# Where a block's gradient rows are stored in the backward chain of a memory-augmented attention kernel

## The chip, the cores and the metric

The kernel runs on one core of one Trainium2 chip. A core has TensorE (PE, matrix products), VectorE (DVE), ScalarE (ACT), GpSimd (POOL) and SyncE (SP). SP computes nothing: it issues DMAs, one after another, in the order of its program. POOL issues DMAs too. The metric is the device time of one execution in microseconds (us); lower is better.

## What is computed

The reference is the forward pass of two summed branches and its gradients by automatic differentiation: a recurrent attention with a memory of 8 rows that is carried from one segment of 32 rows to the next, and a dense layer with a squared ReLU. The attention branch, cut to what matters (its gradient runs the same chain from the last segment to the first):

```python
for s in range(n_seg):                       # 2048 / 32 = 64 segments
    h = jnp.concatenate([mem, x[:, s*32:(s+1)*32, :]], axis=1)   # 8 + 32 rows of 512
    q, k, v = (jnp.einsum('btd,dhe->bhte', h, W) for W in (Wq, Wk, Wv))  # 32 heads of 128
    p = _softmax(jnp.where(mask, jnp.einsum('bhqe,bhke->bhqk', q, k) * scale, -1e9))
    o = jnp.einsum('bhte,hed->btd', jnp.einsum('bhqk,bhke->bhqe', p, v), Wo)
    mem = o[:, :M, :]
    outs.append(o[:, M:, :])
...
_out, _vjp = jax.vjp(_f, A_x, A_mem0, A_Wq, A_Wk, A_Wv, A_Wo, B_w1, B_b1, B_w2, B_b2)
_grads = _vjp(grad_out)
```

All inputs are bfloat16.

## The kernel before

The program runs in five parts one after the other: the dense branch, the forward chain over 64 segments, the backward pass of the memory rows of all blocks with the rest of the dense branch's weight gradients, the backward chain over 64 segments, and the weight gradients of the attention. The change lies in the backward chain.

One step of the backward chain is one segment. Four segments make a block (16 blocks), and the chain goes from the last block to the first. A step needs the gradient of the memory rows that the step before it made, so the steps are a chain. Within a step (`bwd`, L1314):

- `o0mm`, `o1mm`: the output gradient times Wo (L374), two halves of the heads; `o0ev`, `o0te` and so on: its casts and turns.
- `vp0`, `vp1` (L1384): gradient rows of the values; `vea`, `veb` (ACT) cast them into `G4["v"]`, called gv in the profile; `vla`, `vlb` cast the part that belongs to the memory rows.
- `s0`, `s1`, `d10` to `d41`: score gradients, on DVE.
- `kp0`, `kp1` and `qp0`, `qp1` (both L626, through `outer`): gradient rows of keys and queries. `kp` reads b_qN, the step's query rows; `qp` reads b_kN, its key rows, and b_kNL, the key rows of the block's memory (L1340, loaded once for each block in two halves by `ldk0`, `ldk1`; one buffer). `kea0` ... `qeb1` cast the results into `G4["k"]` and `G4["q"]`, gk and gq.
- `vg`, `kg`, `qg` (L495): these rows times the weights, summed over the heads into the gradient of the segment's rows.

gv, gk and gq hold the rows of all four steps of a block, in one buffer each. When a block is done they are stored whole in S_GB, for the last part of the program. Each is stored by two DMAs of 512 KB: the values by groups of heads, so that both DMAs need all eight heads of each group (`vo0`, `vo1`), keys and queries by heads 0 to 3 and 4 to 7 of each group (`ko0`, `ko1`, `qo0`, `qo1`). The next block's casts into the same buffer wait until the stores have read it.

The order is written out by hand. `B_ORDER` (L1156) has four strings, for the first to the last step of a block; `play` (L655) calls the named pieces in that order, and every engine keeps the order of the calls that fall to it. A plus sign shifts a name by one step; names with `L.` belong to a block and a plus shifts them by one block. In the first string, `L.ko1+` means the block that was finished with the step before; in the fourth string, `L.vo0++` means the block whose last step is running. `ldk0+++` in the first string loads b_kNL for the step that is running. Since no engine waits for another except through data, SP can run ahead of PE, and waits at the first DMA whose data or buffer isn't ready.

Other DMAs on SP's queue in a block's last step and in the next first step: `vtr` (L1344, a transposing load of b_vl, the next step's values), `L.ldt` (L635, the same for the memory's values, b_vTL), `L.qtr` (L1277, transposes b_gqL into gNat), `L.lq` (L1219, loads the next b_gqL into the same buffer), `L.qst` (L1286, stores gNat in S_GL), `L.sx` (L1289). On POOL's queue are `ldp`, `ldq`, `ldn` (L1330, L1337, L1338: b_P, b_qN, b_kN of a step), `ldv` and `ldk` (L1303 to L1308: PGD, b_gOL, b_GL, b_qNL of a block).

SP has eight semaphores for its DMAs, used in turn: each issue also waits until the DMA eight before it has landed.

Of the kernel before, what the change touches and what calls it, by code (L numbers as in the profile page):

```python
# [26 lines left out]
def kernel(  # L27
# [35 lines left out]
    L = M + SEG  # L63
# [146 lines left out]
    with sb("p1b", 2) as p1b, sb("p1", 1) as p1:  # L210
# [90 lines left out]
        for rb in range(NRB):  # L301
# [38 lines left out]
            xb = xq[rb]  # L340
# [310 lines left out]
    def on_engines(act, vec):  # L651

        return dict([(n, acp) for n in act.split()] + [(n, vcp) for n in vec.split()])
# [338 lines left out]
    with sb("la", 2) as la, sb("ls", 2) as ls, sb("lo", 1) as lo_, sb("wg", 2) as wg, psum("lpp", 1) as lpp, psum("lr", 4) as lr:  # L992
# [161 lines left out]


    B_ORDER = (  # L1156
# [6 lines left out]
        "pb+++ rb+++ ldq+++ L.H2+ ta+++ tb+++ vc+++ Ha+++ Hb+++ o0mm++++ o0ev++++ o1mm++++ o1ev++++ xb+++ o0fl++++ "  # L1163
# [10 lines left out]
        "ta++++ rb++++ Ha++++ tb++++ Hb++++",  # L1174
# [5 lines left out]
        "ta++++ L.qst+ kla1++++ tb++++ L.H0++ Ha++++ Hb++++")  # L1180
    ENGS = on_engines(
        "L.ra0 kea0 keb0 keb1 kla0 kla1 o0ev o1ev qea0 qea1 qeb0 ra vea veb vla vlb",
        "kea1 klb0 klb1 o0te o1te qeb1")
# [501 lines left out]
```

## Time and profile before

| | |
|---|---|
| median of 3 runs | 2894.07 us (2890.13 to 2901.47) |
| the profiled execution | 2889.67 us, of which the span 2887.9 us |
| granted clock of TensorE, mean over the span | 0.975 |
| busy share of the span | PE 93%, DVE 44%, ACT 35%, POOL 23% |
| moved by DMA | 586.77 MB, mean 203 GB/s |
| the queue of SP, share of 16 engines | 68.7% |
| the queue of POOL, share of 16 engines | 15.0% |
| the backward chain in the span | 1344.6 us (first o0mm) to about 2291 us |

The profile shows one execution. "Busy" is the time in which an engine ran instructions; the DMA share is the mean busy share of the core's 16 DMA engines. PEclk is the clock that TensorE was granted, 1.00 being full. A wait is told as the engine and line that waited, an arrow, and what ended it, with total us, number of times and the longest. In a timeline a line has its start, its length, the engine (SPq: SP's queue, that is issues of DMAs), the source line, the operation and out<-in; a bracket behind it tells how long the engine was idle before it.

### The profile page before, as it was taken

The numbers are of one execution on the slowest core, as the hardware profiler recorded it, in microseconds if no ns is written. First come the engines' busy times: TensorE is split into PE (matmuls) and PEld (weight loads), VectorE is DVE, ScalarE is ACT, GpSimd is POOL, SyncE is SP. The second block draws the span as 40 slices with busy tenths as digits, with TensorE's granted clock in tenths as the row PEclk, the third lists the DMA queues.
The fourth block names the chain that finished last, engine by engine and source line by source line (L and its number), as shares of the span: only waits on it lengthen the run. The fifth ranks groups of instructions, "written<-read, shape, count | busy, mean of one in ns | idle before, by whom it ended". The sixth has DMA issues, their size and how long they took to land.

```text
span 2887.9 us, 117038 instructions
## 1 busy us (share of the span) xinstructions
PE 2682.9 (93%) x52405; PEld 1446.5 (50%) x52405; DVE 1277.6 (44%) x3755; ACT 1002.5 (35%) x2330; POOL 662.5 (23%) x1284
## 2 busy tenths in 40 slices
PE   7998999999999997988998989989999898999999
PEld 3444555555555555455554545544554443444444
DVE  4544666666666664444454445544554401100000
ACT  2323444444444445232433333333433311111111
POOL 1001000000000001223443333433343323322221
PEclk9999999999999998998999999999999999999999
DMA  9764589899989998996677767786778799999993
GB/s 249 265 206 157 158 192 220 211 215 222 219 201 225 212 214 220 288 245 168 160 177 213 179 169 178 187 207 166 178 175 211 236 247 201 213 206 243 208 212 75
DMA packets 837275, 586.77 MB, mean 203 GB/s; under 512 B 637938, under 2 KB 723459, under 8 KB 833443
## 3 DMA queue, kind: packets, MB, share of 16 engines
q1 hardware_dynamic: 794642, 451.83, 68.7%
q0 software_dynamic: 41984, 127.32, 15.0%
q8 instruction: 411, 6.73, 1.0%
q14 instruction: 94, 0.76, 0.1%
q10 hardware_dynamic: 144, 0.13, 0.0%
HBM read 184.95 MB, written 248.79 MB: 150 GB/s over the span
## 4 chain that ended last, share of the span: by engine, by line
PE 78%; DMA 7%; SPq 6%; issue 4%; DVE 4%; ACT 1%; POOL 1%; ACTq 0%; DVEq 0%; POOLq 0%
PE ps_proj L374 15%; PE ps_gw L1643 14%; PE ps_gR L495 11%; PE ps_R L495 5%; SPq L1524 3%; PE ps_tr L167 3%; PE ps_L L374 3%; PE b_pp L626 3%; PE ps_RL L1254 3%; DMA b_qN<-S_A 2%; PE ps_sc L467 2%; PE f_pp L626 2%; PE ps_w L1104 2%; PE ps_B L345 2%; PE ps_gxb L354 2%
## 5 line engine op out<-in xcount | busy, mean ns | idle before, releaser
L1643 PE MATMUL ps_gw<-gn,HNc 128*128 128x512 bf16 x1920 | 422.1, 382 | 12.6 <-DMA gn<-S_GL 6.5
L1643 PEld LDWEIGHTS <-HNc 128*128 128x128 bf16 x1920 | 188.6, 98 | 240.7 <-issue 11.3
L422 ACT CAST f_N<-ps_proj 128x512 bf16<-128x512 f32 x320 | 184.1, 581 | 196.3 <-PE ps_proj L374 191.0
L1577 ACT CAST wt<-ps_gw 128x512 bf16<-128x512 f32 x128 | 73.8, 588 | 458.8 <-PE ps_gw L1643 419.7
L374 PEld LDWEIGHTS <-X 128*32 128x32 bf16 x5760 | 144.3, 96 | 136.7 <-DVE X L540 21.0
L1560 DVE TENSOR_TENSOR gx<-ps_rows,gb 128x512 f32<-128x512 f32 x16 | 11.1, 691 | 422.2 <-PE ps_rows L1558 422.2
L887 POOL COPY kM<-f_kT 128x256 bf16<-128x256 bf16 x64 | 25.8, 402 | 744.4 <-DVE f_kT L425 569.9
L495 PE MATMUL ps_gR<-Wv,gv 128*32 128x512 bf16 x2048 | 143.8, 402 | 6.8 <-issue 6.8
L495 PE MATMUL ps_gR<-Wk,gk 128*32 128x512 bf16 (+1 forms) x2048 | 139.4, 384 | 6.2 <-issue 5.2
L1643 PE MATMUL ps_gw<-GOc,gn 128*128 128x512 bf16 x640 | 139.2, 379 | 1.4 <-DMA GOc<-in_grad_out_dram 1.3
L495 PE MATMUL ps_R<-Wo,OT 128*32 128x256 bf16 x4096 | 128.6, 277 | 4.2 <-issue 2.8
L422 ACT CAST gON<-ps_proj 128x512 bf16<-128x512 f32 x128 | 75.0, 586 | 159.2 <-PE ps_proj L374 159.2
L1578 POOL DMA_DIRECT2D out_dram<-wt x120 | 64.9, 542 | 281.5 <-ACT wt L1577 266.3
L495 PE MATMUL ps_gR<-Wq,gq 128*32 128x512 bf16 (+1 forms) x2048 | 124.4, 351 | 5.0 <-issue 5.0
L374 PE MATMUL ps_proj<-Wo,GT 128*32 128x512 bf16 x2048 | 123.9, 384 | 5.3 <-DVE GT L1299 5.2
L374 PE MATMUL ps_proj<-Wq,X 128*32 128x512 bf16 x1920 | 127.3, 382 | 1.3 <-issue 1.3
L374 PE MATMUL ps_proj<-Wk,X 128*32 128x512 bf16 x1920 | 124.2, 382 | 1.1 <-issue 0.5
L422 ACT CAST gk<-b_pp 128x256 bf16<-128x256 f32 x192 | 69.2, 379 | 157.9 <-PE b_pp L626 96.4
L374 PE MATMUL ps_proj<-Wv,X 128*32 128x512 bf16 x1920 | 121.5, 378 | 0.0
L1335 POOL COPY PD<-b_P 32x320 bf16<-32x320 bf16 x256 | 115.4, 451 | 9.9 <-PE ps_tr L167 1.2
L1330 POOL DMA_DIRECT2D b_P<-S_A x63 | 33.8, 537 | 364.5 <-issue 136.1
L495 PEld LDWEIGHTS <-OT 128*32 128x32 bf16 x4096 | 104.6, 98 | 11.8 <-issue 5.7
(291 smaller groups left out, 5284.5 us busy)
## 6 DMA issues: line engine op xcount, KB each, us to landing
S_A<-f_N SPq DMA_DIRECT2D x64, 512.0 KB
out_dram<-wt POOLq DMA_DIRECT2D x134, 128.0 KB, 5.5
S_A<-f_N SPq DMA_DIRECT2D x64, 256.0 KB
S_GB<-gv SPq DMA_DIRECT2D x32, 512.0 KB
S_GB<-gk SPq DMA_DIRECT2D x32, 512.0 KB
S_GB<-gq SPq DMA_DIRECT2D x32, 512.0 KB
b_kN<-S_A POOLq DMA_DIRECT2D x63, 256.0 KB, 4.3
b_qN<-S_A POOLq DMA_DIRECT2D x63, 256.0 KB, 3.7
```

The costliest lines, as they stand in the source:

```text
L167: nc.tensor.transpose(ps_ap, in_ap, ident[base:base + k, base:base + k])
L345: nc.tensor.matmul(psB[:], lhsT=aT[:, fc, rc * P:(rc + 1) * P], rhs=W2[:, fc, :], start=(fc == 0), stop=(fc == FC - 1))
L374: nc.tensor.matmul(o, lhsT=hT[:, dc, :], rhs=x, start=(dc == 0), stop=(dc == DC - 1), tile_position=(0, 32 * g))
L422: nc.scalar.copy(out, in_)
L495: nc.tensor.matmul(R[32 * g:32 * g + 32, 0:(cs.stop - cs.start) * P].rearrange("p (a b) -> p a b", b=P), lhsT=XT(k, g), rhs=x[:, cs, :], s ...
L626: nc.tensor.matmul(o, lhsT=N_[32 * g:32 * g + m, kk * P:(kk + 1) * P], rhs=X(kk)[32 * g:32 * g + m], start=(i == 0), stop=(i == len(jobs) ...
L1254: nc.tensor.matmul(ps["R", i][32 * g:32 * g + 32, :].rearrange("p (a b) -> p a b", b=P), lhsT=B_[n][:, k, g, :], rhs=W(g * KH + k), start= ...
L1335: nc.gpsimd.tensor_copy(PD[32 * g:32 * g + 32, g], C["P"][32 * g:32 * g + 32, :, KW - L:KW])
L1524: nc.sync.dma_start_transpose(got[i][q][:, x, :].rearrange("p (k e) -> p k e", k=KH), S_GB[4 * q + x, t][:, g].rearrange("p k r -> p (k r)"))
L1577: nc.scalar.copy(wt[:], ps[:])
L1578: eng(dst, wt[:])
L1643: nc.tensor.matmul(ps[:], lhsT=l(rc), rhs=r(rc), start=(n == 0), stop=(n == RC_ALL - 1))
```

## The change

Six names move in `B_ORDER`; nothing else is touched.

```diff
     B_ORDER = (
-        "L.vo0+ o0mm++++ o1mm++++ L.vo1+ o0ev++++ pb+++ xa+++ L.xt ldk0+++ o1ev++++ o0fl++++ xb+++ L.ra0+ vp0++++ "
-        "o0te++++ L.G2+ ldk1+++ vea++++ s0++++ d10++++ o1fl++++ d20++++ L.ko0+ d30++++ vla++++ o1te++++ vp1++++ "
-        "ldn+++ L.I1+ L.G1+ d40++++ ldp++++ ldq+++ veb++++ s1++++ d11++++ vlb++++ kp0++++ ldp+++++ vg1++++ L.qo0+ "
-        "tu0++++ L.qo1+ keb0++++ d21++++ qp0++++ kla0++++ L.sx+ vg0++++ kea0++++ d31++++ qeb0++++ d41++++ vtr++++ "
-        "L.ko1+ kg0++++ klb0++++ tu1++++ qp1++++ ldn++++ qeb1++++ qea0++++ qg0++++ qea1++++ kp1++++ qg1++++ keb1++++ "
+        "o0mm++++ o1mm++++ L.ko1+ o0ev++++ pb+++ xa+++ L.xt ldk0+++ o1ev++++ o0fl++++ xb+++ L.ra0+ vp0++++ "
+        "o0te++++ L.G2+ ldk1+++ vea++++ s0++++ d10++++ o1fl++++ d20++++ d30++++ vla++++ o1te++++ vp1++++ "
+        "ldn+++ L.I1+ L.G1+ d40++++ ldp++++ ldq+++ veb++++ s1++++ d11++++ vlb++++ kp0++++ ldp+++++ vg1++++ "
+        "tu0++++ keb0++++ d21++++ qp0++++ kla0++++ L.sx+ vg0++++ kea0++++ d31++++ qeb0++++ d41++++ vtr++++ "
+        "kg0++++ klb0++++ tu1++++ qp1++++ ldn++++ qeb1++++ qea0++++ qg0++++ qea1++++ kp1++++ qg1++++ keb1++++ "
...
-        "vlb++++ d40++++ d11++++ vg0++++ kp0++++ L.tb+ kla0++++ tu0++++ d21++++ qp0++++ vg1++++ d31++++ keb0++++ "
+        "vlb++++ d40++++ d11++++ vg0++++ kp0++++ L.vo0++ L.vo1++ L.tb+ kla0++++ tu0++++ d21++++ qp0++++ vg1++++ d31++++ keb0++++ "
         "d41++++ kea0++++ kg0++++ kp1++++ L.qtr+ qeb0++++ tu1++++ L.G0++ klb0++++ qp1++++ L.ldv++ L.ta+ qea0++++ "
-        "qg0++++ qeb1++++ kea1++++ keb1++++ qea1++++ kg1++++ L.lq++ klb1++++ qg1++++ L.I0++ ra++++ L.ldk++ rb++++ "
-        "ta++++ L.qst+ kla1++++ tb++++ L.H0++ Ha++++ Hb++++")
+        "qg0++++ qeb1++++ kea1++++ L.qo0++ keb1++++ qea1++++ kg1++++ L.lq++ klb1++++ qg1++++ L.I0++ ra++++ L.ldk++ L.qo1++ rb++++ "
+        "ta++++ L.qst+ L.ko0++ kla1++++ tb++++ L.H0++ Ha++++ Hb++++")
```

On SP's queue this makes, from a block's last step into the next first step:

- before: vtr, ldt, qtr, lq, qst, **vo0, vo1**, ldk0, ldk1, **ko0, qo0, qo1**, sx, vtr, **ko1**
- after: vtr, ldt, **vo0, vo1**, qtr, **qo0**, lq, **qo1**, qst, **ko0, ko1**, ldk0, ldk1, sx, vtr

POOL's order and the order of work on PE, ACT and DVE stay as they are.

## The prediction

> **What bounds the kernel now.** The page gives PE 93% of the span and 78% of the chain that ended last, so only idle or slow stretches of PE can be won or lost. I first cut the backward chain into its 64 steps, at the first output-projection matmul of each step in the PE timeline, and asked for busy times by stretch. Here are the last step of one block, the three first steps of the next block, and 7 us around the border between the blocks:
>
> ```profile
> core 0: us, PE busy (x) PEld busy (x) DVE busy (x) ACT busy (x) POOL busy (x), PEclk, DMA share, GB/s
> 1446.55:1462.42 15.87, 13.85 (x362) 7.57 (x365) 8.00 (x24) 5.50 (x15) 8.38 (x16) 1.00 0.88 252
> 1462.42:1479.76 17.34, 14.66 (x369) 7.71 (x361) 6.95 (x24) 6.03 (x16) 4.25 (x8) 0.90 0.64 181
> 1479.76:1493.11 13.35, 13.23 (x358) 7.27 (x358) 7.92 (x23) 5.35 (x15) 5.36 (x12) 1.00 0.54 139
> 1493.11:1505.68 12.57, 12.40 (x350) 6.93 (x349) 6.32 (x21) 5.63 (x15) 4.39 (x9) 1.00 0.51 128
> 1458.00:1465.00 7.00, 7.00 (x133) 3.89 (x136) 2.50 (x10) 1.92 (x5) 2.21 (x5) 1.00 0.97 335
> ```
>
> Second and third steps take 13 us and PE hardly stops. First steps take 13.8 to 20.9 us, 17.6 on average over the fifteen that follow another block; last steps 15.3. At the border the DMA engines are full: 335 GB/s at a share of 0.97. From here on I call the start of a block's first step zero; -5 is 5 us before it.
>
> Then the chain of waits, at another block's first step:
>
> ```profile
> 1518.29 0.48 POOL b_kN L1338
> 1518.78 0.52 POOL b_P L1330
> 1519.29 7.07 DMA b_qN<-S_A
> 1526.41 0.35 PE b_pp L626 x28
> 1526.76 2.16 issue
> ```
>
> A load of 256 KB takes 7 us to land there (its shortest landing is 2.8, its median 3.7), and PE waits for it; behind it come 2.16 us of "issue", in which PE waited for nothing that the profile shows. Over the chain, the waits for this load and for the gradient stores are:
>
> ```profile
> PE b_pp L626 <- DMA b_qN<-S_A: 15.4, 9, 3.7
> ACT gk L422 <- DMA S_GB<-gk: 12.3, 7, 2.6
> ACT gv L422 <- DMA S_GB<-gv: 4.5, 2, 3.2
> ```
>
> Last, the SP queue at the first of the two borders (zero is 1462.42), up to the first load behind the stores that PE needs:
>
> ```profile
> 1445.55 1.68 SPq L635 DMA_TRANSPOSE b_vTL<-S_NL  x1
> 1447.28 1.37 SPq L1277 DMA_TRANSPOSE gNat<-b_gqL  x1
> 1450.84 0.33 SPq L1219 DMA_DIRECT2D b_gqL<-S_GQL  x1
> 1451.22 0.43 SPq L1286 DMA_DIRECT2D S_GL<-gNat  x1
> 1451.69 0.96 SPq L1241 DMA_DIRECT2D S_GB<-gv  x2
> 1456.33 0.81 SPq L1340 DMA_DIRECT2D b_kNL<-S_NL  x2
> 1457.24 0.56 SPq L1241 DMA_DIRECT2D S_GB<-gk  x1
> 1457.85 2.04 SPq L1241 DMA_DIRECT2D S_GB<-gq  x2
> 1463.65 0.34 SPq L1289 DMA_DIRECT2D S_XG<-b_XT  x1
> 1464.10 1.51 SPq L1344 DMA_TRANSPOSE b_vl<-S_A  x1
> 1465.99 0.56 SPq L1241 DMA_DIRECT2D S_GB<-gk  x1
> ```
>
> The reader is to see two things. SP runs ahead of PE: the value stores already go out at -10.7, inside the last step, whatever line of the order they stand in. And the two loads of b_kNL, which the first step's qp0 needs, go out ahead of four of the six stores.
>
> **The change, part by part.** No instruction is added or removed; POOL keeps its order, and the compute engines theirs. Only SP's queue changes. For one block it becomes: transposes of b_vl and b_vTL, both value stores, transpose of b_gqL, first query store, load of b_gqL, second query store, S_GL store, both key stores, both b_kNL loads, S_XG, the next b_vl.
>
> *Value stores ahead of the transpose.* They need the last gv cast, which ends at -11.0 on average (ACT timeline, fifteen borders). Two issues of 0.5 us put the transpose at -10; here it was at -15.1. The load of b_gqL waits for that transpose to land, because it overwrites what the transpose reads (3.6 us here, up to 6.8 elsewhere), and behind it on SP now stand five stores and the b_kNL loads. Before, the value stores stood behind it too, but four of the six stores stood behind b_kNL. So: 1.05 MB of value stores, then about 2 us of transpose (between two transposes' packets in the DMA records; equal to 0.6 MB), with about 0.45 MB of POOL's loads in between, make 2.1 MB; at 0.33 MB/us (the 335 GB/s above) 6.4 us. I split the 2 us of the shortest landing that are not moving data in two halves, 1 before and 1 after: the packets start at -10.4, end at -4, the transpose lands near -3. The fuller queue slows its packets somewhat; I take -2.5.
>
> *b_kNL behind all six stores.* From about -3.5, these have to go before its first half is in: two query stores, two key stores (2.1 MB), b_gqL and S_GL (0.52), the half itself (0.13), and from POOL's queue, which shares the engines, b_GL, b_qNL, b_kN, b_P and b_qN (1.05). That is 3.8 MB or 11.5 us: 8, and 1 more to land, 9, with a little of PE's own start 9.5. qp0 starts today at 7.4, 6.4, 11.0, 10.6, 7.4, 7.4, 8.5, 6.6, 10.7, 8.5, 6.4, 9.6, 7.6, 7.3 and 6.4 (PE timeline). The parts above 0 of 9.5 minus these add up to 24.6 us: **+24**. Bounds: 0, when b_kNL lands by 6.4; +55, when PE is let go at 11.8 (same sum). I stay near the middle because the bytes are counted.
>
> *Waits for the stores.* gv and gk are overwritten by the next block's first step. 12.3 + 4.5 us of ACT's waits stand above, and DVE has 4.5 more for gk: 21 us. Those near 16 (late second key store, 1.6, 1.2 and 1.8 us) reach PE and end; the first key store lands later than now and keeps its waits: **-5**, bounds -21 and 0.
>
> *Unexplained stops of PE.* After qp0's start there are 14 of over 0.2 us in the fifteen first steps, 24.2 us together; second steps have none at a DMA share of 0.55. They go with full DMA engines. The second key store, now at 3.6 to 10.5, goes before zero, so after qp0's later start about 3 us of full engines remain where 5 were: 24.2 x 2/5, **-9**, bounds -24 and 0.
>
> *The clock.* Nine of the fifteen first steps have a granted clock of 0.82 to 0.91; one minus clock, times length, adds up to 18.7 us, 1.7 for the usual stretch. The row above has 0.90 after one stop of 2.63 us (1469.02 to 1471.65). A wait of 2 to 3 us at nearly every border brings four more: **+7**, bounds 0 and +10.
> The Trainium skill ("TensorE: Matmul & The Clock Gate", Part 1: The HAM clock gate) has the half clock come after a whole idle window of about 3.4 us. By that rule the new waits alone would cost no clock (a rival below); the trace throttled after 2.63 us, so I go by the trace.
>
> *At nothing:* b_qN, since POOL's share of the engines stays (15.4 us to win; as much to lose if SP's fuller queue slows it). The b_gqL load, read only in the next second step, after 18: some 14 us of cover. The next b_vl, which will land near 13, is read by POOL's copy at 16.4 (1478.86): 3 us of cover, past which each late us costs up to 15. The last block's stores: their readers start at 2380.
>
> Sum: 24 - 5 - 9 + 7 = **+17 us** on the profiled 2889.67 (span 2887.9 and 1.8 around it), 2906.7. The median of the runs shown is 4.4 above that execution, inside their spread of 2890 to 2901; for a median I give 2894 + 17 = **2911**.
>
> **The rivals.**
> *No change* (2896). SP already ran ahead, so the stores move by a few us only and the same bytes cross the same border. b_kNL then lands by 8, which leaves 9 us of the first term against -5, -9 and +7. For it: the byte counts are equal. Against: b_kNL passes from in front of four stores to behind them.
> *No clock lost* (2904): as forecast, but stops of 2 to 3 us leave the clock alone, 24 - 5 - 9 = +10. For it: the stop of 1.54 us in the first step at 1639.85 cost none (1.00). Against: the 0.90 after 2.63 us.
> *Faster* (2868): the border is bound by the tail of stores, not by b_kNL. Value stores land by -5 (up to 6.2 now), no key store is left after 7, so PE's stops fall by 24, the gk waits by 5, and the clock is lost half as often (-9): -38, with +12 for a b_kNL that is somewhat late. It decides as soon as b_kNL lands within 7.5. For it: today's slow windows start near 9 to 12, just where the second key store runs. Against: the sum above, which needs 2 MB less ahead of b_kNL.
> *Much slower* (2945): b_kNL at 11.8 (+55) with +7 for the clock, less 11 of the gains. For it: SP's own issues stretch to 4 us under load, and one b_vl transpose issue here took 4.04 (1700.65). Against: the rate was 335 GB/s where nothing was short.
>
> **Numbers.** Chances: forecast 0.40 (own range 2909 to 2930), no change 0.22, no clock lost 0.05, faster 0.20, much slower 0.13. Half a per cent, 14.5 us, is about what a measurement of this kernel tells from none. Slower 0.53, same 0.27 (both small cases), faster 0.20. The range, 2872 to 2940, takes in most of both outer cases.
>
> **What would show it.** Right: PE waits at L626 for b_kNL, 1 to 3 us at most borders; b_kNL issued after the key stores, near 0; waits of ACT for S_GB<-gv gone; first steps near 18.7; more of them below 0.95 of the clock; second and third steps as before. Wrong: no wait for b_kNL and first steps under 17; or b_vl late, seen as POOL's copy waiting for it and second steps longer than 13.

## The result, and the profile after

Over 19 executions of each kernel the changed one takes 2901.4 us in the median (2885.25 to 2921.85) and the one before 2891.19 (2871.31 to 2901.8). The ratio is 1.0048, 95% interval [1.0029, 1.0067]: about 14 us slower (0.0048 x 2891); the two medians lie 10.2 us apart. The forecast was +17 us. The ratios here and below leave out executions over 1.5% above the fastest of the same kernel, such as one of 8740.21 us in e2. The profiled execution of the changed kernel took 2891.01 us (span 2889.2), 10 below its median, so its length says little; its parts say more.

The same border as in the forecast, by stretch (last step of a block, then the three first steps of the next):

```profile
core 0: us, PE busy (x) PEld busy (x) DVE busy (x) ACT busy (x) POOL busy (x), PEclk, DMA share, GB/s
1445.20:1461.85 16.65, 13.81 (x361) 7.53 (x364) 8.00 (x24) 5.50 (x15) 8.45 (x17) 1.00 1.00 233
1461.85:1477.00 15.15, 13.58 (x368) 7.50 (x360) 6.96 (x24) 6.03 (x16) 4.26 (x8) 1.00 0.79 228
1477.00:1490.36 13.36, 13.24 (x359) 7.28 (x358) 7.92 (x23) 5.35 (x15) 5.35 (x12) 1.00 0.53 138
1490.36:1503.10 12.74, 12.48 (x349) 7.01 (x348) 6.36 (x22) 5.63 (x15) 4.56 (x9) 1.00 0.68 134
```

The last step is 0.8 us longer than before, the first step 2.2 shorter, and the second and third are within 0.2 us of what they were. The DMA engines are now full in the last step (share 1.00, before 0.88). Over all fifteen borders of the profiled pair, last steps went from 15.27 to 16.07 us in the mean, first steps from 17.57 to 16.42. So the borders did not get slower, though the kernel did.

SP's queue at this border:

```profile
1449.55 0.82 SPq L1241 DMA_DIRECT2D S_GB<-gv  x2
1450.42 2.17 SPq L1277 DMA_TRANSPOSE gNat<-b_gqL  x1
1453.12 0.56 SPq L1241 DMA_DIRECT2D S_GB<-gq  x1
1457.92 0.33 SPq L1219 DMA_DIRECT2D b_gqL<-S_GQL  x1
1458.35 0.54 SPq L1241 DMA_DIRECT2D S_GB<-gq  x1
1458.94 0.62 SPq L1286 DMA_DIRECT2D S_GL<-gNat  x1
1459.61 2.13 SPq L1241 DMA_DIRECT2D S_GB<-gk  x2
1461.85 1.96 SPq L1340 DMA_DIRECT2D b_kNL<-S_NL  x2
```

b_kNL goes out at zero, behind all six stores, as forecast. SP stands for more than 4 us (from 1453.7 to 1457.92) before the b_gqL load, until the transpose has landed.

The waits in the backward chain and up to the first weight gradients:

```profile
PE ps_RL L1254 <- DMA b_gqL<-S_GQL: 15.6, 1, 15.6
PE b_pp L626 <- DMA b_kNL<-S_NL: 11.1, 10, 1.2
PE b_pp L626 <- ACT gk L422: 10.0, 6, 2.5
PE ps_RL L1254 <- ACT gNat L422: 8.2, 1, 8.2
...
PE b_pp L626 <- DMA b_qN<-S_A: 3.8, 2, 2.5
...
ACT gk L422 <- DMA S_GB<-gk: 27.1, 11, 3.9
```

Two kinds of lines are new. At the borders PE waits ten times for b_kNL, 1.2 us at most, and six times for a gk cast that waits for a store; the waits for b_qN fell from 15.4 to 3.8. And two single long waits, 15.6 and 8.2 us, stand at one place: after the last block of the chain. The chain of waits there (the last step of the chain starts at 2271.2):

```profile
2276.61 23.93 DMA gNat<-b_gqL
2300.58 0.06 issue
2300.64 0.33 SPq L1219
...
2301.62 15.27 DMA S_GL<-gNat
2317.20 0.59 ACT gNat L422
...
2325.79 0.38 PE ps_gw L1643
```

The first line is the transpose of b_gqL, now issued behind the value stores: 23.93 us to land, where it took 7 to 8 at most borders. L1219, the b_gqL load, has to wait for it; the S_GL store behind it takes another 15.27 us, and the last part of the program starts its first weight-gradient matmul (L1643) at 2325.79. Before, SP's queue at the same place (last step from 2276.4) was this:

```profile
2272.05 1.23 SPq L1277 DMA_TRANSPOSE gNat<-b_gqL  x1
2277.99 0.32 SPq L1219 DMA_DIRECT2D b_gqL<-S_GQL  x1
2278.35 0.98 SPq L1286 DMA_DIRECT2D S_GL<-gNat  x1
2280.74 1.10 SPq L1241 DMA_DIRECT2D S_GB<-gv  x2
```

and the first weight-gradient matmul stood at 2306.42: 30.0 us after the start of the last step, and with the change 54.6. Most of these 24.6 us come back: from that matmul to the end the changed kernel takes 563.5 us and the one before 581.5, with 12.6 us of stops of PE and 8.6 us lost to the clock (17 us at half clock), because its loads (S_GB, S_GL) were then late instead. From the start of the last step to the end: 611.5 before, 618.0 changed.

### The profile page after: what moved, and what is told of

It reads as the page before. It is cut to its first block, busy times and chain, and to the rows that moved or that the text cites. A ratio compares the mean times of both kernels' runs of the same rounds, so it can differ in the third digit from the quotient of the medians.

```text
span 2889.2 us, 116959 instructions
## 1 busy us (share of the span) xinstructions
PE 2677.2 (93%) x52314; PEld 1449.5 (50%) x52405; DVE 1277.4 (44%) x3755; ACT 1002.5 (35%) x2330; POOL 662.9 (23%) x1284
## 3 DMA queue, kind: packets, MB, share of 16 engines
q0 software_dynamic: 41984, 127.32, 15.1%
q8 instruction: 411, 6.73, 1.0%
## 4 chain that ended last, share of the span: by engine, by line
PE 81%; DMA 8%; DVE 4%; issue 3%; SPq 2%; ACT 1%; POOL 0%; ACTq 0%; DVEq 0%; POOLq 0%
PE ps_gw L1643 19%; PE ps_proj L374 15%; PE ps_gR L495 11%; PE ps_R L495 4%; PE ps_tr L167 3%; PE b_pp L626 3%; PE ps_L L374 3%; PE ps_RL L1254 3%; DMA b_kNL<-S_NL 3%; PE f_pp L626 2%; PE ps_sc L467 2%; PE ps_w L1104 2%; PE ps_B L345 2%; PE ps_gxb L354 2%; PE b_T L531 2%
## 5 line engine op out<-in xcount | busy, mean ns | idle before, releaser
L1643 PE MATMUL ps_gw<-gn,HNc 128*128 128x512 bf16 x1883 | 414.9, 379 | 1.9
L1643 PEld LDWEIGHTS <-HNc 128*128 128x128 bf16 x1920 | 187.9, 98 | 223.6
L1560 DVE TENSOR_TENSOR gx<-ps_rows,gb 128x512 f32<-128x512 f32 x16 | 11.1, 692 | 423.6 <-PE ps_rows L1558 423.6
L1643 PE MATMUL ps_gw<-GOc,gn 128*128 128x512 bf16 x626 | 138.4, 379 | 2.0 <-issue 1.3
```

Of the source, the lines that this page charges most:

```text
L1643: nc.tensor.matmul(ps[:], lhsT=l(rc), rhs=r(rc), start=(n == 0), stop=(n == RC_ALL - 1))
```

## The experiments

The theory: the loss is at the end of the chain, where no next step covers the b_gqL load; the borders cost nothing. The rival: the loss is at the borders, through b_kNL and the key stores. Twelve runs, five rounds each; every ratio is to the kernel before, executed in the same session. "End" below is the time from the start of the chain's last step to the end of the span; "borders" the sum of the fifteen last and fifteen first steps. Both come from the PE timeline of each run's profiled execution, and a border sum varies from one execution to the next by some 10 us.

### Four corners: borders and last block changed separately (e1, e2, e10, e11, e12)

In e1 and e11 the last block (b = 0) keeps the places of before, under names with z; in e2 and e12 it is the other way round. e10 is the changed kernel again.

```diff
-                    o["%so%d" % (n, x)] = so
+                    o["%s%s%d" % (n, "o" if b > 0 else "z", x)] = so
...
-        "o0mm++++ o1mm++++ L.ko1+ o0ev++++ ...
+        "L.vz0+ o0mm++++ o1mm++++ L.vz1+ L.ko1+ o0ev++++ ...
```

(and so on for the other four names). Expected of e1 and e2:

> The changed kernel, but the last block of the chain (it has no next block) stores its rows at the places of before; the other fifteen borders are as changed. Theory (the loss is at the end of the chain, where b_gqL's transpose took 23.9 us to land and the load behind it had no cover): from the chain's last step to its first weight-gradient matmul (L1643) the time is as before, that matmul stands some 19 us earlier against the chain's last step than in the changed kernel, and the kernel is 0 to 9 us faster than before (ratio 0.997 to 1.000), since the borders gave 5 us in the profiled pair. Rival (the loss is at the borders: PE's waits for b_kNL and for the gk casts behind the late key stores): the ratio stays at 1.004 to 1.006.

> The kernel before, but the last block of the chain alone stores as changed; the fifteen borders are as before. Theory (end of the chain): the b_gqL load of the last block is issued 15 to 25 us later than before, the first weight-gradient matmul stands 15 to 20 us later against the chain's last step, and the ratio is 1.003 to 1.007 (some of it given back in the last part, where PE stopped about 10 us before). Rival (borders): ratio within 0.001 of 1, since the borders are untouched.

Expected of their repetition:

> The changed kernel once more, beside the two half-changed ones, so that the end of the chain and the fifteen borders can be told apart in four corners. Theory (end of the chain): ratio 1.003 to 1.007, 618 to 619 us from the start of the last step to the end. Rival (the first interval was an accident of its pairing): 1.000 to 1.003.

> Borders as changed, last block as before, once more. Theory: 609 to 612 us after the start of the last step, ratio 0.997 to 1.001, and 0.003 to 0.007 under the changed kernel of this call. Rival (the borders carry the loss): within 0.002 of the changed kernel.

> Borders as before, last block as changed, once more. Theory: 618 to 619 us after the start of the last step, ratio 1.002 to 1.007. Rival (the first figure, 1.0070, was high by chance and the end costs little): ratio 0.999 to 1.001.

Measured:

| borders | last block | ratio to before, 95% interval | end, us |
|---|---|---|---|
| before | before | 1 | 611.5 |
| changed | before (e1, e11) | 0.9999 [0.9969, 1.0028]; 1.0006 [0.9979, 1.0034] | 609.5; 604.2 |
| before | changed (e2, e12) | 1.0070 [1.0039, 1.0101]; 1.0057 [1.0035, 1.0080] | 618.9; 619.0 |
| changed | changed (first comparison, e10) | 1.0048 [1.0029, 1.0067]; 1.0045 [1.0021, 1.0069] | 618.0; 618.2 |

SP's queue at the end of the chain in e12, where nothing but the last block is changed (its last step starts at 2280.0):

```profile
2284.34 0.82 SPq L1241 DMA_DIRECT2D S_GB<-gv  x2
2285.20 5.60 SPq L1277 DMA_TRANSPOSE gNat<-b_gqL  x1
2290.85 2.07 SPq L1241 DMA_DIRECT2D S_GB<-gq  x1
2309.34 0.33 SPq L1219 DMA_DIRECT2D b_gqL<-S_GQL  x1
```

The load goes out 29.3 us after the last step's start, before the change 1.6. The theory held: the last block alone makes the kernel slower, the fifteen borders alone don't. Averaged over the four corners the last block is worth +0.0054 (16 us; the mean of 0.0063 with the borders of before and 0.0044 with the changed ones), the borders -0.0007 (-2 us). The ends in the profiles differ by 10 us (618.5 against 608.4, the means of four and three); the rest lies within the intervals. That e1 might be up to 9 us faster than before was not borne out. In e2 the first weight-gradient matmul stood 25.5 us later than before against the last step, not 15 to 20, and the end of e11 was shorter than the 609 to 612 expected.

### b_kNL ahead of the key stores (e3)

```diff
-... L.xt ldk0+++ o1ev++++ ... L.G2+ ldk1+++ vea++++ ...
+... L.xt o1ev++++ ... L.G2+ vea++++ ...
...
-... kg1++++ L.lq++ klb1++++ ...
+... kg1++++ ldk0++++ ldk1++++ L.lq++ klb1++++ ...
```

> The changed kernel with both loads of b_kNL issued in the block's last step, ahead of the b_gqL load and so ahead of the second query store and both key stores. Theory: PE's waits for b_kNL (11.1 us in the profiled run) go, b_kNL lands by 4 us after zero instead of 5.4 to 10.3; the key stores move back by half a us or so, so waits of the gk casts stay or grow; first steps get shorter by up to 0.7 us each. The end of the chain stays as late as in the changed kernel, so the kernel is 0 to 11 us faster than the changed one (ratio to before 1.001 to 1.005). Rival (all of the loss is b_kNL): ratio 1.000 or lower. Second rival (what b_kNL frees, the gk casts take): ratio as the changed kernel's, 1.004 to 1.006.

Ratio 1.0052 [1.0022, 1.0082]: the changed kernel's, so the second rival came true. b_kNL landed at -0.1 in the mean (8.3 in the changed kernel), and no wait for it is left:

```profile
PE ps_RL L1254 <- DMA b_gqL<-S_GQL: 15.0, 1, 15.0
PE b_pp L626 <- ACT gk L422: 9.1, 5, 2.3
...
PE b_pp L626 <- DMA b_qN<-S_A: 7.5, 4, 3.4
```

But the unexplained stops of PE in the first steps are 21.0 us here, where the five profiles with the changed borders have 4.4 to 15.9 (10.7 in the mean). It was not the gk casts that took what b_kNL freed (9.1 us, 10.0 in the changed kernel); the stops did.

### What the unexplained stops are (e8)

The forecast had put them down to the second key store in the middle of the first step. e8 is the kernel before with that store alone moved, right behind the first:

```diff
-... L.ko0+ d30++++ ...
+... L.ko0+ L.ko1+ d30++++ ...
...
-        "L.ko1+ kg0++++ klb0++++ ...
+        "kg0++++ klb0++++ ...
```

> The kernel before with the second key store alone moved: right behind the first, instead of 3 to 10 us into the next first step. Theory F (the stops of PE in the first steps are late instruction fetches; they vanished in the changed kernel because PE waited for b_kNL while the fetch came): stops stay at 1.4 to 2.3 us per first step, first steps within 0.4 us of those before, ratio 0.998 to 1.002; each stop of over 0.8 us ends 1.2 to 1.5 us after a 16 KB packet of the instruction queue has come in. Rival S (the second key store in the middle of the first step makes the stops, as the prediction had it): stops fall below 0.7 us per first step, first steps 1 us or more shorter, ratio 0.993 to 0.996.

Ratio 0.9985 [0.9954, 1.0015]. The stops in first steps were 25.6 us together (1.7 each), before 31.5: theory F. So the second key store does not make most of them. What the stops are shows in the packet records of one queue (a line of the changed kernel's page: packets, MB, share of 16 engines):

```profile
q8 instruction: 411, 6.73, 1.0%
```

These are 411 packets of 16,384 bytes, 6.73 MB. PE's 52,314 matmuls and 52,405 weight loads make 255 instructions for each packet, so this queue seems to carry PE's program. In the fourteen profiled executions there are 253 stops of over 0.8 us in the chain that nothing explains, and 243 of them end 1.15 to 1.75 us after such a packet has come in; of moments drawn at random 11 to 12% do. 240 of the 253 stand in last and first steps and none in a second step, where the mean DMA share is 0.57 to 0.60 (last steps 0.88 to 1.01, first steps 0.71 to 0.85); 13 stand in third steps. In the 3 us before such a packet starts the share is 1.08 in the median, before the chain's other packets 0.69. A packet itself takes about 1 us in all steps alike (median 0.99 in first steps before the change, 0.99 in second and third), but at a stop it starts when PE is some 130 instructions further than usual (before the change, median 471 against 339 instructions beyond 255 for each earlier packet). So, as the traces read, PE has run out of instructions: the packet is not slow, it starts late, and this happens where the DMA engines are full. No run changed the instruction queue alone. The Trainium skill ("Runtime: NRT & Kernel Launch", Instruction fetch mechanics) says that programs are refilled in blocks of 16 KiB or 256 instructions and that the cost of a block's border is mostly hidden. The block's size agrees with the trace; here it is not hidden, with up to 47 us of unexplained stops in the thirty border steps of one execution (e5).

This would also explain e3: while PE waits for b_kNL, the next block of instructions comes in; take the wait away and PE stops for the instructions instead. The fourteen profiles agree. Where PE does not wait for b_kNL at all (six of them) the first steps have 19.3 to 34.5 us of unexplained stops; with 3.4 us of that wait (e5) 23.2; with 7.0 to 9.0 us 12.5 to 15.9; with 10.4 to 11.5 us 4.4 to 9.6.

### The transpose's place (e4, e6, e7)

e4 is the changed kernel with the transpose of b_gqL ahead of the value stores again:

```diff
-... kp0++++ L.vo0++ L.vo1++ L.tb+ ... kp1++++ L.qtr+ qeb0++++ ...
+... kp0++++ L.qtr+ L.vo0++ L.vo1++ L.tb+ ... kp1++++ qeb0++++ ...
```

> The changed kernel with the transpose of b_gqL ahead of the value stores again, as it stood before. Theory: at the end of the chain the transpose lands within 7 us, the b_gqL load goes out near the chain's end as before and the first weight-gradient matmul is back to where it was (some 15 to 19 us earlier against the last step than in the changed kernel); at the borders the transpose goes out some 4 us earlier, and the value stores land a little later, so border steps stay within 0.3 us of the changed kernel's. Ratio to before 0.996 to 1.001. Rival (loss at the borders): ratio 1.003 to 1.006.

In e6 only the last block has its value stores behind the transpose; e7 is the kernel before with the two value stores alone at their new place.

> The changed kernel, but in the last block alone the value stores stand behind the transpose of b_gqL; the fifteen borders are as changed. Theory (what the transpose's place is worth is worth it at the end of the chain only): from the start of the last step to the end 604 to 606 us (618.0 changed, 611.5 before), ratio to before 0.996 to 0.998, the same as with the transpose first everywhere. Rival (part of that gain came at the borders): ratio 0.999 to 1.002.

> The kernel before with the two value stores alone moved to their new place; key and query stores and b_kNL as before. Theory (a transpose behind the value stores loses the end of the chain, whatever the other four do): the last block's transpose takes over 15 us to land, the end stands 617 to 620 us after the start of the last step, and the borders are as before (PE stops that nothing in the profile explains, 1.5 to 2.5 us per first step; no waits for b_kNL): ratio 1.001 to 1.006. Rival (the loss needs the key and query stores ahead as well): the end at 609 to 612 us, ratio 0.998 to 1.001.

| run | ratio, 95% interval | end, us |
|---|---|---|
| e4, transpose first everywhere | 0.9959 [0.9933, 0.9986] | 604.6 |
| e6, transpose first in the last block | 1.0009 [0.9982, 1.0035] | 608.5 |
| e7, values alone | 0.9997 [0.9969, 1.0025] | 610.4 |

e4 is 12 us faster than before (0.0041 x 2891), at the fast edge of the expectation, but the theory was wrong on where: e6 has the same order at the last block (its end is 10 us shorter than the changed kernel's) and is 0.0050 behind e4, so these 0.0050 come from the borders. e9 below, with e4's borders, is 0.0049 under e11, which has the changed borders; their last blocks differ in the place of the second key store alone. At e4's borders the waits of PE for gk are gone, and ACT's for the key stores fell from 27.1 to 13.3, while those for b_qN, 3.8 in the changed kernel, are 12.0:

```profile
PE b_pp L626 <- DMA b_qN<-S_A: 12.0, 8, 2.4
PE b_pp L626 <- DMA b_kNL<-S_NL: 10.4, 10, 2.4
PE ps_RL L1254 <- ACT gNat L422: 9.1, 1, 9.1
```

e7 missed. Its last transpose took 24 us to land as well, and its b_gqL load went out as late as the changed kernel's (29.6 us after the last step's start, there 29.4), but the first weight-gradient matmul came 46.9 us after that start (54.6 in the changed kernel), and the end was 610.4, no later than before. So the late transpose and load alone cost nothing that its end or its ratio shows. In e7 no query or key store stands between the transpose and the load of b_gqL or the S_GL store, and that store landed 8.79 us after its issue, in the changed kernel 15.27: most of the 8 us between the two. Which of the moved stores makes it late was not tried.

Why the first part of the delay is free can be read from the fourteen profiles. Where the first weight-gradient matmul comes 28.7 to 30.4 us after the last step's start, the rest takes 569.7 to 581.5 us; where it comes at 41 or later, 563.5 (565.5 in e6). Starting earlier mostly moves the wait to the last part's loads.

### Two attempts at a better kernel (e5, e9)

e5 is e4 with the b_gqL load right behind the value stores; e9 is e4 at the borders, with the last block as before the change but its second key store behind the first.

```diff
-... L.qtr+ L.vo0++ L.vo1++ L.tb+ ... kg1++++ L.lq++ klb1++++ ...
+... L.qtr+ L.vo0++ L.vo1++ L.lq++ L.tb+ ... kg1++++ klb1++++ ...
```

> The run with the transpose of b_gqL ahead of the value stores, and now also the b_gqL load right behind the value stores instead of behind the first query store. Theory (the end of the chain): the load of the last block goes out by about 3 us after the start of the last step (8.4 in that run, 1.6 before the change), the first weight-gradient matmul stands 30 to 36 us after the start of the last step (41.1 there, 30.0 before, 54.6 changed), and from there to the end it takes 563.5 us as in that run and in the changed kernel: 5 to 10 us faster than that run, ratio to before 0.992 to 0.995. Rival: once the weight-gradient part starts earlier, its first loads are late as they were before the change (581.5 us from there to the end, with 13.9 us of stops of PE), and the total stays at 0.996 to 0.999.

> The run with the transpose first for the fifteen borders; the last block as before the change, but with its second key store right behind the first. Theory: the two parts add up: from the start of the last step to the end 600 us (604.6 with the transpose first, 600.0 with the key store early), so 3 to 6 us under the run with the transpose first: ratio to before 0.992 to 0.996. Rival (the 0.9959 of the transpose first was partly chance, since the same tail under the changed borders gave 1.0009): ratio 0.996 to 0.999.

e5: 0.9973 [0.9944, 1.0001], end 605.6. The last block's load went out at 5.4 and the first weight-gradient matmul stood at 42.2, no earlier than in e4 (41.1): the load is not all that it waits for there (a single wait of 11.9 us for gNat's cast). e9: 0.9957 [0.9932, 0.9983], end 609.0: as fast as e4, no faster. The end of 600.0 in e8 did not come again in e9 with the same places, and e11 had 604.2 with the places of before, so ends with an early b_gqL load vary from 600 to 612 between executions, while those of the changed last block were 618.0 to 619.2 in all five. The ratio lies where the two ranges meet. That e4's gain was partly chance, as the rival had it, is not borne out, since e9 shows it again; but the other last block added nothing to it.

```profile
2260.69 1.24 SPq L1277 DMA_TRANSPOSE gNat<-b_gqL  x1
2265.86 0.32 SPq L1219 DMA_DIRECT2D b_gqL<-S_GQL  x1
2266.22 1.66 SPq L1286 DMA_DIRECT2D S_GL<-gNat  x1
2269.44 1.67 SPq L1241 DMA_DIRECT2D S_GB<-gv  x2
```

This is SP's queue at the end of the chain in e9: transpose, load and S_GL store go out within 6 us, ahead of all stores. e4 and e9 are both faster than the kernel before and than the changed one.

### The borders in numbers

Sums over the thirty border steps of one execution, in us: stops of PE of over 0.2 us that nothing explains, stops with a cause (data), and what the half clock took (half the time at half clock).

| run | borders | unexplained, last + first steps | data | clock | both steps |
|---|---|---|---|---|---|
| before | before | 10.0 + 31.5 | 24.0 | 22.2 | 492.6 |
| e2 | before | 11.1 + 34.5 | 25.9 | 35.8 | 508.6 |
| e12 | before | 11.9 + 32.9 | 21.8 | 22.2 | 494.3 |
| changed | changed | 18.7 + 4.4 | 34.4 | 25.6 | 487.4 |
| e1 | changed | 17.9 + 7.9 | 34.2 | 32.4 | 496.8 |
| e10 | changed | 19.2 + 13.0 | 28.8 | 22.2 | 490.1 |
| e11 | changed | 16.2 + 12.5 | 29.8 | 35.8 | 497.7 |
| e6 | changed | 17.8 + 15.9 | 31.5 | 29.0 | 499.4 |
| e3 | b_kNL early | 23.7 + 21.0 | 24.8 | 37.5 | 510.2 |
| e4 | transpose first | 16.9 + 9.6 | 29.3 | 17.1 | 481.0 |
| e9 | transpose first | 14.2 + 12.6 | 24.5 | 15.4 | 476.1 |
| e5 | transpose first, load early | 23.5 + 23.2 | 17.8 | 20.5 | 493.5 |
| e7 | values alone | 20.6 + 19.3 | 20.5 | 15.4 | 485.1 |
| e8 | second key store early | 13.9 + 25.6 | 23.5 | 23.9 | 493.9 |

With the change, unexplained stops fall from 44 to 29 us in the mean, stops for data rise from 24 to 32, and the clock stays (27 and 29): about -5 us together. e4 and e9 have some 7 us less of stops than the changed borders (54 against 60) and lose 13 us less to the clock. Why so little less stopping costs so much less clock is not settled: e7 loses as little clock with 60 us of stops, and e5, with the transpose first as well, has 64.5 and gained less (0.9973). That the transpose's place at the borders is worth some 14 us is shown by the ratios; how, it is not.

## Why the prediction came near, and which step failed

The total was close (+17 forecast, +14 measured) by luck: errors that cancel. In the forecast all 17 us were at the borders; in the runs the borders gave -2 and the last block +16. The median, 2901.4, lies below the forecast's own range of 2909 to 2930; the forecast set out from 2894, and 19 executions of the kernel before gave 2891.19. Of its signs, the order of b_kNL, the waits for it, the gone gv waits and the unchanged second and third steps came; first steps near 18.7 did not (16.4 to 17.2 in the five profiles with the changed borders), and the waits were 1.2 us at most, not 1 to 3, in the first profile.

- *The step that failed: "At nothing: [...] The b_gqL load, read only in the next second step, after 18: some 14 us of cover" and "The last block's stores: their readers start at 2380".* Fifteen blocks have that cover; the last has no next step. There its transpose landed after 23.93 us instead of the 7.5 that the forecast gave it (-10 to -2.5), while the last part's loads fill the DMA engines (between 2275 and 2300 us POOL's queue, which carries them, took 84% of the engines' time), and the load behind it went out 29.4 us after the last step's start, before 1.6. The late load alone does not do it, though: the value stores alone ahead of the transpose (e7) leave the end at 610.4, all six stores moved but behind the transpose (e6) at 608.5, the whole change at 618.0 to 619.2. With the whole change, the S_GL store landed after 15.27 us and the first weight-gradient matmul came at 54.6 us, before 30.0. The forecast looked at the readers of the stores alone, and not at the load and the store that the moved stores delay.
- *b_kNL behind all six stores, +24.* The mechanism was right: the first half landed at 8.1 to 8.5 in the mean of each changed profile, forecast 9. The size was not: PE waited 7.5 to 11.5 us for it in the five profiles, not 24. The term took today's starts of qp0 as given, but, as far as the traces tell, b_qN (11 to 18.8 us of waits with the borders of before, 3.8 to 8.6 with the changed) and the late instructions had made them late, and these left at the same time.
- *b_qN, "at nothing"*: wrong, a gain of some 9 us (15.1 to 6.4 in the means).
- *Waits for stores, -5.* The gv waits went, as forecast. But ACT's waits for the key stores grew from 12.3 to 27.1 us, and PE waited 6.6 to 10.0 us for those casts: a loss of about 8 where a gain stood.
- *Unexplained stops, -9.* Right in sign. In first steps they fell by 22 us (33 to 11), but 7 of them came back in last steps (11 to 18), where the DMA engines are now full: -15. The part given to the second key store fell with e8; that the stops go with full DMA engines held. (24.2 x 2/5 is 9.7, not 9.)
- *Clock, +7.* 27 us lost before, 29 changed, with 22 to 36 from one execution to the next: no difference shown. Of the fifteen first steps nine had lost clock in the profiled execution before, eight after. In this the rival "no clock lost" was right (its 2904 is also the figure nearest to the median), but not in its reason: stops of 1.5 to 2.5 us do cost clock (below).
- *Rivals.* "No change" is what the borders did, though by other terms. The much slower rival and its late b_vl did not occur: second and third steps kept 13.19 and 13.03 us (13.18 and 13.04 before). The faster one needed b_kNL within 7.5; its early b_kNL was tried in e3 and gained nothing.

## What to carry to other kernels

For a DMA moved in a loop, look at the last pass by itself: what covered a late load in every other pass is missing there, and what follows may be filling the same engines (the transpose took 24 us to land there, 7 to 8 at most borders). A load that waits for a transpose to read its buffer stops the whole queue behind it, so here the transpose goes ahead of the bulk stores (e4, e9), not behind; the load right behind the value stores gained nothing more (e5). And removing a named wait pays nothing where an unnamed one stands right behind it: e3 took 9 to 11 us of waits away and had some 10 us more of unexplained stops in the first steps (21.0 against 10.7 in the mean). A late load at the end of a loop need not cost what it delays: look at what the next part then waits for.

## What the runs showed of the hardware

- PE's program seems to come in by DMA, and where the DMA engines are full it comes late: 243 of 253 unexplained stops end 1.15 to 1.75 us after a 16 KB packet of the instruction queue, and 240 stand in last and first steps (mean DMA share 0.71 to 1.01), none in second ones (0.57 to 0.60).
- The clock can fall after short stops. Half-clock stretches in the fourteen profiled chains are 3.4 us long (137 of 172), some 6.8 (34). Of stops of 1.5 to 2.5 us 71 of 136 are followed by one within 3.6 us, of 1.0 to 1.5 us 35 of 160, and of those under 1 us 37 of 610. The Trainium skill ("TensorE: Matmul & The Clock Gate", Part 1: The HAM clock gate) asks for a whole idle window of about 3.4 us; that length agrees with the stretches, but not with what sets them off here.
- One and the same transpose of 256 KB lands after 7 to 8 us at most borders of the changed kernel (5.2 to 10.0) and after 24 where the last part's loads run (23.9 to 24.5 in six runs). SP's later DMAs of the same queue stand behind the one that waits for it.
